# Spectral filter with a two-layer network on one core: two last-stage pieces moved, the first batch's x in five loads, the filter's downward rows first

## The chip, the core and the metric

The kernel runs on one core of a Trainium2 chip. A core has five engines that run at the same time, each with its own list of instructions, and that wait for one another through semaphores: PE (TensorE: matrix products, its weight loads shown apart as PEld), DVE (VectorE), ACT (ScalarE), POOL (GpSimd) and SP (SyncE, here only an issuer of transfers). PE writes into PSUM, a small memory of eight banks; DVE and ACT copy from there to SBUF, the working memory. Transfers between DRAM and SBUF are issued by SP or POOL and carried out by 16 DMA engines. The metric is the time of one execution on the device in microseconds (us).

## The reference

`x` has 8 batches of 3008 positions and 256 channels. It is filtered in the frequency domain along the positions and then sent through a two-layer network with a leaky activation:

```python
X = np.fft.rfft(x, axis=1)
Y = X * (filt_r + 1j * filt_i)[None, :, :]
y = np.fft.irfft(Y, n=x.shape[1], axis=1)
g = y.reshape(B * S, D) @ w_in                      # 256 -> 2048
g = np.maximum(g, 0.0) + alpha * np.minimum(g, 0.0)
out = g @ w_out                                     # 2048 -> 256
```

## The kernel before, in words

The transform of length 3008 = 94 * 32 is done as two layers of small matrix products, and so is its inverse. Matrix operands are fp16; `x` and the filter are turned from fp32 to fp16 by the DMA that loads them, and only POOL issues such DMAs.

The network (`class Block`) takes 512 positions at a time (one block of each pair of batches has 384). `up` multiplies by `win_s` into a two-bank PSUM tile `hps`; ACT copies it to `gtb` (L569; L591 in `up4`), and DVE makes `m` (L572, L596) and adds it to `gtb` (L574, L597). `down` multiplies by `wout_s` (L614); ACT copies to `osb`, SP stores. A block is 16 steps, each one `up` and as a rule one unit of `down`. Into these steps the FFT work of the following batches is put by a plan written out by hand: `put(step, fn, ...)` puts a piece ahead of the `up` of that step. The first block has no `down` work yet. It is done as two halves of 256 positions by `up4`: eight calls, at steps 0, 2, ..., 14, the first four for the first half and the last four for the second. `up4` takes functions (`mid`) that are called between its matmuls and its ACT copy.

The first batch has nothing to hide behind, so `class First` does its FFT ahead of the blocks, in this order:

- `load_x` (L116) brings x of a batch in four parts `c` of eight positions each, into four `xs` buffers with 94 rows (partitions) of 2048 values; each part is two DMAs of 48 and 46 rows. `load_filt` (L136) brings the filter in three loads of four of the twelve frequency pairs `kp`, each as eight DMAs: real and imaginary part, two groups `e`, and 16 rows read upward (one contiguous run a row) or 16 rows read downward (step -1, eight runs a row).
- `piece_a(i)`, i = 0 to 7, is the first layer (L337): two pieces for each part `c`. ACT and DVE copy the results to `am`, which is a part of `gtb`.
- `turn_at` (L351) transposes two to four columns of `am` on PE; a copy brings them to `at`.
- `piece_b(kp)` (L363) is the second layer; DVE multiplies its result by the filter, `uu(kp)` (L368). It uses one `hps` buffer, of which there are two, so DVE's products set the pace of `piece_b`.
- `piece_c(kp)` (L389) starts the inverse; `keep_c` copies its result to `v` after every second pair, and after each of the last two.
- `side_t`, `half_t` and `piece_t` (L411, L405) transpose `v` on PE, and a copy brings it to `zt`.
- `half_d` and `pair_d` (L288) are the last stage of the inverse: eight matmuls of `wif_s` for a `pair_d`, four for a `half_d`, and a copy to `yT`, the input of the network. `half_d(0)` to `half_d(3)` give the first 752 positions and `pair_d(2)`, `pair_d(3)` the next 752, one half of the channels each. `pair_d` uses `psF`, a PSUM tile of which there is one buffer.

`warm(n, bank)` (L452) puts n matmuls of the identity into PE's list, whose results nobody reads; they fill PE's time. Each has one weight load and 512 columns.

The transfers of the network's weights `win_s` and `wout_s` and of x of the second batch are issued by POOL in the loop over `kp`, at `kp == 4`; the first of them waits for a DVE memset on `win_s`, which stands behind `uu(6)` in DVE's list. POOL's DMAs take eight semaphores in turn, so that each waits until the DMA eight places earlier has landed.

Of the kernel before, what the change touches and what calls it, by code (L numbers as in the profile page):

```python
# [14 lines left out]
N1 = 94  # L15
N2 = 32
NK = 24
D = 256
# [37 lines left out]
def kernel(  # L56
# [10 lines left out]
    nc = tc.nc  # L67
# [28 lines left out]
    filt_s = konst.tile([128, 12, 2, D], FP16, name="filt_s")  # L96
# [15 lines left out]
    def xrow(b, c):  # L112
        return bass.AP(tensor=x.tensor, offset=x.offset + (b * NFFT + 8 * c) * D,
                       ap=[[N2 * D, N1], [1, 8 * D]])

    def load_x(b, c, held=False):  # L116
        xs = p_x.tile([128, 8 * D], FP16, name="xs")
        if held:
            for r in (slice(0, 32), slice(64, 96)):
                nc.vector.memset(xs[r, 0:2], 0.0)  # L120
        for r in (slice(0, 48), slice(48, N1)):
            nc.gpsimd.dma_start(out=xs[r], in_=xrow(b, c)[r])  # L122
        return xs

    def load_halves(b, c):
# [7 lines left out]
            nc.gpsimd.dma_start(out=hi[32:47], in_=xrow(b, c)[79:94])  # L133
        return lo, hi

    def load_filt(eng, dst, ha, hb, parts=(0, 1)):  # L136
        n = hb - ha
        for i in parts:
            src = (filt_r, filt_i)[i]
            for e in range(2):  # L140
                q = 64 * e + 32 * i
                k = 2 * ha + 24 * e
                for j, step, off in ((0, 1, k), (16, -1, N1 - k)):
                    eng.dma_start(  # L144
                        out=dst[q + j : q + j + 16, ha:hb].rearrange("p h r d -> p (h r) d"),
                        in_=bass.AP(tensor=src.tensor, offset=src.offset + off * D,
                                    ap=[[N1 * D, 16], [step * D, 2 * n], [1, D]]))

    def banks(wide):
        if wide:  # L150
            return psH.tile([128, 2, 512], FP32, name="hps")
        return psF.tile([128, 2, 512], FP32, name="psF")

    def bank(kind):
        if kind == "o":
            return psO.tile([128, 2, D], FP32, name="op").rearrange("p k d -> p (k d)")
        return banks(kind == "h")[:, 0]
# [151 lines left out]
    def on_act(o, i):  # L309
        nc.scalar.activation(o, i, AF.Copy)  # L310

    def on_dve(o, i):
        nc.vector.tensor_copy(o, i)  # L313
# [116 lines left out]
    def table(ka, kb):  # L430
        nc.sync.dma_start(out=twf_s[:, ka:kb], in_=consts["twf"].ap()[:, ka:kb])

    def inverse_table(ka, pb):
        for i in range(4):
            nc.tensor.matmul(pb[:, 128 * i : 128 * i + 128],
                             twf_s[:, ka + 2 * i : ka + 2 * i + 2].rearrange("p k m -> p (k m)"), id16,
                             start=True, stop=True)
        on_act(twi_s[:, ka : ka + 8].rearrange("p k m -> p (k m)"), pb)

    def swapped(ka, eng):  # L440
        t, o = twi_s[:, ka : ka + 8], twx_s[:, ka : ka + 8]
        eng.tensor_scalar(o[:, :, 32:64], t[:, :, 0:32], gs_s, None, OP.mult)
        eng.tensor_scalar(o[:, :, 0:32], t[:, :, 32:64], gs_s, -1.0, OP.mult, OP.mult)

    xc = {(0, c): load_x(0, c) for c in range(4)}
    f0 = First()
    table(0, 8)
    load_filt(nc.gpsimd, filt_s, 0, 4)

    def warm(n, pw):  # L450
        for _ in range(n):
            nc.tensor.matmul(pw.rearrange("p (r c) -> p r c", r=4), id16,  # L452
                             id16.unsqueeze(1).to_broadcast([128, 4, 128]), start=True, stop=True)

    warm(10, bank("o"))
    for i in range(8):
        f0.piece_a(i, i % 3 < 2)
        if i == 3:
            inverse_table(0, bank("o"))
            swapped(0, nc.vector)  # L460
            warm(3, bank("o"))
        elif i % 2 == 1:
            warm((8, 0, 6, 0)[i // 2], bank("o"))
        if i in (5, 7):
            ka = 4 * i - 12
            nc.vector.memset(twf_s[:, ka : ka + 8, 0:1], 0.0)
            table(ka, ka + 8)
    load_filt(nc.gpsimd, filt_s, 4, 8)
    warm(3, bank("o"))
    f0.turn_at(0, 1, on_act)  # L470
    f0.turn_at(1, 1, on_dve, True)
    warm(2, bank("o"))
# [1 line left out]
    f0.turn_at(2, 2, on_act)  # L474
    f0.piece_b(1)
    inverse_table(8, bank("o"))
    load_filt(nc.gpsimd, filt_s, 8, 12)
    nc.gpsimd.memset(twi_s[:, 16:24, 0:1], 0.0)
    swapped(8, nc.gpsimd)
    nc.gpsimd.tensor_copy(id32, ids[0:16, 0:16])  # L480
# [7 lines left out]
    nc.sync.dma_start(out=twi_s[:, 16:24], in_=consts["twj"].ap())  # L488
    nc.sync.dma_start(out=twx_s[:, 16:24], in_=consts["twy"].ap())
    for kp in range(12):  # L490
        if 0 < kp < 9:
            f0.piece_b(kp + 2)
        if kp == 8:
            f0.piece_b(11)
        if kp == 4:
            nc.vector.memset(win_s[:, :, 0:1], 0.0)
            for kt in range(2):
                nc.gpsimd.dma_start(out=win_s[:, kt], in_=moe_w_in[kt * 128 : (kt + 1) * 128])
            xc[(1, 0)] = load_x(1, 0)
            for q in range(2):  # L500
                nc.gpsimd.dma_start(
                    out=wout_s[:, 8 * q : 8 * q + 8],
                    in_=moe_w_out[1024 * q : 1024 * q + 1024].rearrange("(j p) d -> p j d", p=128))
            for c in range(1, 4):
                xc[(1, c)] = load_x(1, c)
        f0.piece_c(kp)
        if kp > 9:
            f0.keep_c(kp, (on_act, on_act) if kp == 10 else both, 1)
        elif kp % 2 == 1:
            f0.keep_c(kp - 1, (on_act, on_act))  # L510
            if kp < 7:
                f0.turn_at(kp + 5, 2, on_act)
        if 7 < kp < 10:
            warm(2, banks(False)[:, 0])
    for o in range(0, 128, 64):
        for i in range(0, 64, 32):
            nc.gpsimd.dma_start(out=filts_s[o + i : o + i + 32], in_=filt_s[o + 32 : o + 64])
# [3 lines left out]
    on_act(*f0.side_t(0))  # L521
    on_dve(*f0.side_t(1))
    later = [f0.half_t(2, "h"), f0.half_t(3, "f")]
    f0.half_d(0, on_dve, "o")
    f0.half_d(2, on_act, "o")

    sizes = [512] * 5 + [384] + [512] * 6
    blocks = []
# [96 lines left out]
    def put(step, fn, *args):  # L625
        plan.setdefault(step, []).append((fn, args))
# [41 lines left out]
    put(1, f0.piece_t, 2, on_dve)  # L668
    for i in (6, 7):
        put(3, lambda i=i: on_dve(*f0.half_t(i, "o")))  # L670
    put(5, f0.pair_d, 2, on_dve)
    put(7, f0.pair_d, 3, on_dve)
    for g, ts, ds, te, de in ((2, (19, 23), (25, 28), (on_dve, on_dve), (on_dve, on_dve)),
                              (3, (32, 34), (43, 49), (on_act, on_act), (on_act, on_act))):
        for i in range(2):
# [16 lines left out]
    for b in range(3, NB):  # L692
        p = 96 * (b - 1)
# [20 lines left out]
    for step in range(16):  # L714
        if step % 2 == 0:
            blk.up4(step // 2 % 4, step // 8,
                    [] if step else [lambda: on_dve(*later[0]), lambda: on_act(*later[1]), slopes])
        for fn, args in plan.pop(step, ()):
            fn(*args)
    blk.start_down(False)  # L720
    units.extend((blk, q) for q in range(16))
    step = 16

    for p, t0, tn in blocks[1:]:
        blk = Block(p, t0, tn)
        for j in range(16):
            n = psum.get(step, 0)
# [50 lines left out]
```

## Time and profile before

| | us |
|---|---|
| median of 3 runs (770.80 to 771.02) | 771.01 |
| the profiled execution | 771.15 |
| its span, first to last instruction | 769.4 |
| PE busy in the span (99%) | 758.3 |
| DVE busy (82%) | 633.5 |
| ACT busy (76%) | 582.7 |
| POOL busy (19%) | 147.0 |

The profile gives the span of one execution. A timeline row has the start and the busy time in us, the engine, the line, the operation with what it writes and reads, the count of merged instructions, and in brackets the idle time ahead of it with what ended that. A row of the chain of waits has the start, the duration and what the end of the program goes back to at that time. "issue" is time in which an engine waited for nothing that the profile shows. The table gives busy time by stage, from the view by windows:

| stretch, us | PE | DVE | ACT | POOL | granted clock |
|---|---|---|---|---|---|
| 0 to 15: x, first layer | 12.55 | 4.63 | 5.22 | 10.18 | 1.00 |
| 15 to 31: second layer, filter, inverse | 13.46 | 14.37 | 11.08 | 13.25 | 1.00 |
| 31 to 35: to the first `up4` | 3.63 | 2.25 | 2.50 | 0.66 | 1.00 |
| 35 to 43: first block | 7.54 | 5.44 | 5.87 | 2.85 | 1.00 |
| 43 to 57: first and second block | 13.31 | 13.83 | 12.20 | 2.75 | 1.00 |

### The profile page before, as it was taken

Reading aid. Unit: us, or ns where it says so; the run is one execution under the profiler, and the core shown is the slowest. Engines: PE = TensorE matmul, PEld = TensorE weight load, DVE = VectorE, ACT = ScalarE, POOL = GpSimd, SP = SyncE. Lnnn points to the kernel's source line nnn. Section 1 sums busy time; section 2 is a strip of 40 time slices with the busy share of each in tenths; the row PEclk is TensorE's granted clock in tenths of the full one; section 3 lists DMA queues with packets and bytes.
Section 4 is the critical chain, followed back from the end, with each engine's and each line's share of the span. In section 5 each row is a group of like instructions: output and inputs, shape, how many; then the busy total and the mean of one; then the engine's idle time right before and its main releaser. Section 6 shows DMA issues by size and latency. Waiting matters only on the chain.

```text
span 769.4 us, 16586 instructions
## 1 busy us (share of the span) xinstructions
PE 758.3 (99%) x6544; PEld 507.4 (66%) x6544; DVE 633.5 (82%) x1160; ACT 582.7 (76%) x670; POOL 147.0 (19%) x278
## 2 busy tenths in 40 slices
PE   8999999999999999999999999999999999999998
PEld 4666667666666666666666666766666666766666
DVE  3888885889889998899978998999877888666663
ACT  3787788888778787887778777787767777776664
POOL 7621560122211211121202222022101212000000
PEclk9999999999999999999999999999999999999999
DMA  9996896664843549533783538644463223510111
GB/s 158 165 233 166 138 209 193 168 169 122 201 133 90 138 130 197 153 87 93 187 217 83 132 101 173 178 98 118 125 159 94 69 71 96 152 36 28 42 42 56
DMA packets 97150, 100.04 MB, mean 130 GB/s; under 512 B 12100, under 2 KB 83412, under 8 KB 96880
## 3 DMA queue, kind: packets, MB, share of 16 engines
q1 hardware_dynamic: 82384, 69.50, 31.2%
q0 software_dynamic: 14688, 29.49, 21.3%
q8 instruction: 51, 0.84, 0.4%
q14 instruction: 27, 0.22, 0.1%
HBM read 55.02 MB, written 46.66 MB: 132 GB/s over the span
## 4 chain that ended last, share of the span: by engine, by line
PE 92%; DVE 3%; DMA 2%; ACT 1%; POOL 1%; issue 1%; ACTq 0%; DVEq 0%; POOLq 0%
PE op L614 42%; PE hps L560 41%; PE psF L288 3%; PE hps L266 2%; PE psF L235 1%; DMA xs<-in_x_dram 1%; PE hps L181 1%; PE hps L207 1%; DVE gtb L597 1%; DVE zt L313 1%; ACT asb L310 1%; DVE m L596 1%; DMA filt_s<-in_filt_r_dram 1%; POOL filt_s L144 1%; DMA filt_s<-in_filt_i_dram 1%
## 5 line engine op out<-in xcount | busy, mean ns | idle before, releaser
L569 ACT ACTIVATE gtb<-hps 128x1024 f16<-128x1024 f32 (+1 forms) x376 | 377.6, 1007 | 134.3 <-PE hps L560 130.5
L614 PE MATMUL op<-wout_s,gtb 128*128 128x256 f16 x3008 | 431.3, 273 | 0.0
L560 PE MATMUL hps<-yT,win_s 128*128 128x512 f16 (+1 forms) x1504 | 418.4, 375 | 0.9 <-ACT asb L310 0.3
L614 PEld LDWEIGHTS <-gtb 128*128 128x128 f16 x3008 | 290.9, 98 | 164.2 <-issue 10.7
L572 DVE TENSOR_SCALAR m<-gtb,alm_s 128x512 f16<-128x512 f16 (+1 forms) x752 | 226.9, 345 | 99.4 <-ACT gtb L569 98.0
L574 DVE TENSOR_TENSOR gtb<-gtb,m 128x2048 f16<-128x2048 f16 (+1 forms) x188 | 226.1, 1202 | 10.4
L560 PEld LDWEIGHTS <-win_s 128*128 128x128 f16 x1504 | 142.4, 98 | 55.2 <-issue 6.0
L249 POOL DMA_DIRECT2D sw<-ww x144 | 71.6, 506 | 414.5 <-DVE ww L242 408.7
L619 ACT ACTIVATE osb<-op 128x512 f32<-128x512 f32 (+1 forms) x97 | 56.6, 583 | 12.3 <-PE op L614 10.9
L310 ACT ACTIVATE asb<-hps 128x1024 f16<-128x1024 f32 (+1 forms) x56 | 56.6, 1019 | 5.6 <-PE hps L181 4.3
L310 ACT ACTIVATE v<-hps 128x1024 f16<-128x1024 f32 (+1 forms) x43 | 43.4, 1010 | 10.8 <-PE hps L266 10.6
L242 DVE TENSOR_TENSOR ww<-psF,filts_s 128x1024 f16<-128x1024 f32 x42 | 51.1, 1217 | 0.2 <-PE psF L235 0.2
L243 DVE TENSOR_TENSOR uu<-psF,filt_s 128x1024 f16<-128x1024 f32 x42 | 51.0, 1213 | 0.0
L310 ACT ACTIVATE yT<-psF 128x752 f16<-128x752 f32 x58 | 46.1, 795 | 2.0 <-PE psF L288 1.9
L288 PEld LDWEIGHTS <-zt 96*128 96x128 f16 x512 | 28.5, 98 | 7.2 <-issue 1.2
L288 PE MATMUL psF<-wi_s,zt 96*128 96x94 f16 x448 | 27.9, 205 | 0.1
L247 POOL DMA_DIRECT2D uu<-ww x24 | 19.7, 1241 | 31.5 <-DVE uu L243 23.3
L254 DVE TENSOR_TENSOR uu<-uu,sw 128x1024 f16<-128x1024 f16 x36 | 24.5, 681 | 0.6 <-issue 0.4
L122 POOL DMA_DIRECT2D xs<-in_x_dram x32 | 21.7, 910 | 13.2 <-PE hps L560 4.9
L191 DVE TENSOR_TENSOR xs<-xs 47x2048 f16<-47x2048 f16 x16 | 19.5, 1219 | 0.4
L195 DVE TENSOR_TENSOR xs<-xs 47x2048 f16<-47x2048 f16 x16 | 19.3, 1209 | 0.0
L266 PE MATMUL hps<-uu,twi_s 64*64 64x256 f16 x336 | 17.3, 281 | 0.0
(93 smaller groups left out, 259.9 us busy)
## 6 DMA issues: line engine op xcount, KB each, us to landing
out_dram<-osb SPq DMA_DIRECT2D x128, 128.0 KB
v_dram<-v SPq DMA_DIRECT2D x84, 128.0 KB
zt<-v_dram SPq DMA_DIRECT2D x28, 384.0 KB
sw<-ww POOLq DMA_DIRECT2D x144, 64.0 KB, 2.6
xs<-in_x_dram POOLq DMA_DIRECT2D x44, 192.0 KB, 6.4
at<-a_dram SPq DMA_DIRECT2D x40, 192.0 KB
a_dram<-asb SPq DMA_DIRECT2D x32, 192.0 KB
a_dram<-asb SPq DMA_DIRECT2D x12, 384.0 KB
```

Source lines behind the costliest of these rows:

```text
L242: nc.vector.tensor_mul(ww, px, fs)
L243: nc.vector.tensor_mul(uu, px, f)
L249: nc.gpsimd.dma_start(out=sw[o : o + 32], in_=ww[i : i + 32])
L266: nc.tensor.matmul(ps[64 * par : 64 * par + 64, e, 256 * h : 256 * h + 256], twi_s[r, 4 * q + 2 * h + par], u[r, par, h], start=True, stop ...
L288: nc.tensor.matmul(ps[:, m], self.zt[:, 8 * g + 4 * mh + m, dh * 128 : dh * 128 + 128], self.wi, start=True, stop=True)
L310: nc.scalar.activation(o, i, AF.Copy)
L560: nc.tensor.matmul(self.hps[:, j % 2, 0:tn], win_s[:, kt, j * 128 : (j + 1) * 128], yT[:, kt, self.t0 : self.t0 + tn], start=(kt == 0), st ...
L569: nc.scalar.activation(g[:, 2 * i : 2 * i + 2], self.hps[:, :, 0:tn], AF.Copy)
L572: nc.vector.tensor_scalar(m[:, 2 * i + h], g[:, 2 * i + h], 0.0, a, OP.min, OP.mult)
L574: nc.vector.tensor_add(g, g, m)
L614: nc.tensor.matmul(self.op[:, si - s0], self.gts[k][:, 128 * si : 128 * si + 128], wout_s[:, k], start=(si == s0 and k == 0), stop=(si == ...
L619: nc.scalar.activation(osb[:, 0:m], self.op[:, 0:m], AF.Copy)
```

## The change

It consists of these edits:

1. x of the first batch comes in five DMAs instead of eight: all 94 rows at once, parts 0 to 2 whole and part 3 in two halves of the columns, so that `piece_a(6)` needs only the first of them. The other batches keep the two DMAs of 48 and 46 rows.
2. `load_filt` issues the four DMAs of the downward rows first and then the four of the upward ones; before, they took turns.
3. Four matmuls of `warm` go in the first layer and behind it (6 to 3, and 3 to 2), and four in the loop over `kp` (two each at `kp` 8 and 9).
4. `piece_b(11)` stands at `kp == 9`, behind `piece_c(8)`; before, it stood at `kp == 8` ahead of it.
5. The copies of `half_d(0)` and `half_d(2)` exchange engines: ACT has the first now, DVE the second.
6. `pair_d(2)` goes from step 5 to step 7, behind the fourth `up4`. `pair_d(3)` goes from step 7 into `mid` of the fifth `up4` (step 8), behind that one's matmuls and ahead of its ACT copy. Both are copied by DVE, as before.

```diff
@@ load_x
-        for r in (slice(0, 48), slice(48, N1)):
-            nc.gpsimd.dma_start(out=xs[r], in_=xrow(b, c)[r])
+        if b:
+            for r in (slice(0, 48), slice(48, N1)):
+                nc.gpsimd.dma_start(out=xs[r], in_=xrow(b, c)[r])
+        else:
+            w = 8 * D // (1 + (c == 3))
+            for o in range(0, 8 * D, w):
+                nc.gpsimd.dma_start(out=xs[0:N1, o : o + w], in_=xrow(b, c)[:, o : o + w])
@@ load_filt
-    def load_filt(eng, dst, ha, hb, parts=(0, 1)):
-        n = hb - ha
-        for i in parts:
-            src = (filt_r, filt_i)[i]
-            for e in range(2):
-                q = 64 * e + 32 * i
-                k = 2 * ha + 24 * e
-                for j, step, off in ((0, 1, k), (16, -1, N1 - k)):
-                    eng.dma_start(
-                        out=dst[q + j : q + j + 16, ha:hb].rearrange("p h r d -> p (h r) d"),
+    def load_filt(ha, hb):
+        for j, step, base in ((16, -1, N1), (0, 1, 0)):
+            for i, src in enumerate((filt_r, filt_i)):
+                for e in range(2):
+                    q = 64 * e + 32 * i + j
+                    off = base + step * (2 * ha + NK * e)
+                    nc.gpsimd.dma_start(
+                        out=filt_s[q : q + 16, ha:hb].rearrange("p h r d -> p (h r) d"),
                         in_=bass.AP(tensor=src.tensor, offset=src.offset + off * D,
-                                    ap=[[N1 * D, 16], [step * D, 2 * n], [1, D]]))
+                                    ap=[[N1 * D, 16], [step * D, 2 * (hb - ha)], [1, D]]))
@@ first layer
-            warm((8, 0, 6, 0)[i // 2], bank("o"))
+            warm((8, 0, 3, 0)[i // 2], bank("o"))
...
-    warm(3, bank("o"))
+    warm(2, bank("o"))
     f0.turn_at(0, 1, on_act)
@@ loop over kp
-        if 0 < kp < 9:
+        if 0 < kp < 10:
             f0.piece_b(kp + 2)
-        if kp == 8:
-            f0.piece_b(11)
...
-        if 7 < kp < 10:
-            warm(2, banks(False)[:, 0])
@@ ahead of the blocks
-    f0.half_d(0, on_dve, "o")
-    f0.half_d(2, on_act, "o")
+    f0.half_d(0, on_act, "o")
+    f0.half_d(2, on_dve, "o")
@@ plan
-    put(5, f0.pair_d, 2, on_dve)
-    put(7, f0.pair_d, 3, on_dve)
+    put(7, f0.pair_d, 2, on_dve)
@@ first block
             blk.up4(step // 2 % 4, step // 8,
-                    [] if step else [lambda: on_dve(*later[0]), lambda: on_act(*later[1]), slopes])
+                    {0: [lambda: on_dve(*later[0]), lambda: on_act(*later[1]), slopes],
+                     8: [lambda: f0.pair_d(3, on_dve)]}.get(step, []))
```

More of the change, by code (lines that the diff above doesn't have):

```diff
@@ L447 @@
     table(0, 8)
-    load_filt(nc.gpsimd, filt_s, 0, 4)
+    load_filt(0, 4)
     def warm(n, pw):
@@ L467 @@
             table(ka, ka + 8)
-    load_filt(nc.gpsimd, filt_s, 4, 8)
-    warm(3, bank("o"))
+    load_filt(4, 8)
+    warm(2, bank("o"))
     f0.turn_at(0, 1, on_act)
@@ L476 @@
     inverse_table(8, bank("o"))
-    load_filt(nc.gpsimd, filt_s, 8, 12)
+    load_filt(8, 12)
     nc.gpsimd.memset(twi_s[:, 16:24, 0:1], 0.0)
```

## The prediction, made before the changed kernel was run

> **What bounds the kernel now.** I read the page first, then the chain of waits over 0 to 110 us, then the timeline of the first 60 us engine by engine.
>
> ```profile
> PE 758.3 (99%) x6544; PEld 507.4 (66%) x6544; DVE 633.5 (82%) x1160; ACT 582.7 (76%) x670; POOL 147.0 (19%) x278
> PE   8999999999999999999999999999999999999998
> PEclk9999999999999999999999999999999999999999
> ```
>
> PE is dense in all slices but the first and the last, at full clock. What the change can win lies before the dense part, as an earlier arrival at it; afterwards the same matmuls follow. The chain of waits says what sets that arrival:
>
> ```profile
> 4.96 7.57 DMA xs<-in_x_dram
> ...
> 12.82 1.00 POOL filt_s L144 x2
> ...
> 25.94 0.68 DVE uu L368
> ...
> 42.66 1.15 DVE m L596 x4
> ...
> 57.16 0.49 PE psF L288 x8
> ```
>
> Up to 12.5 us it is the x transfer, then filter transfers, then the filter products `uu` on DVE, a mixed stretch of PE, ACT and DVE, DVE to 57.16, then PE. Two rows of the timeline fix the first joint:
>
> ```profile
> 12.82 0.53 POOL L144 DMA_DIRECT2D filt_s<-in_filt_i_dram  x1 [0.46 <-DMA xs<-in_x_dram]
> ...
> 16.87 9.15 DVE L368 TENSOR_TENSOR uu<-hps,filt_s 128x1024 f16<-128x1024 f32 x8 [1.09 <-PE hps L363]
> ```
>
> The eighth filter DMA is issued at 12.82, when the eighth x DMA has landed (12.53); it lands 3.9 us after issue, at 16.7, and DVE starts `uu(0)` at 16.87. The row names PE, but its `hps` was done at 15.92: the last releaser is the filter. From there twelve products run 1.14 us apart without a gap and end at 30.55.
>
> **Part 1: loads and the first filter load.** POOL's DMAs wait for the one eight places earlier (with eight x loads, filter k waits for x k). With five x loads, filters 1 to 3 wait for nothing, and the eighth waits for x load 5, the last. POOL saves three issues of 0.54 us (L122), at nothing: x is bound by the transfer (1.0 us a load against 0.54 of issue); uncovered they would be worth 1.6. Bytes are the same, and a 48-row and a 46-row load give most engines three packets each, a 94-row load six. So the last x lands at 12.5 again (12.4 to 12.7; the last two loads have 2 KB rows), and the eighth filter is again issued at 12.8. What changes is what it is: an upward one, one 4 KB packet (0.32 us in the packet records) per engine instead of eight of 512 B (0.06 each, 0.48), with the seven before it in the queue earlier. Its first engines cannot land before 15.1, as now (issue plus 2.3); only the tail to 16.7 can shrink. (The Trainium skill, "DMA: Bandwidth & Descriptors", on the anatomy of one DMA, fits about 2.0 us plus bytes over 436 GB/s; as an estimate by that page 64 KB lands 2.15 after issue, at 15.0, and part 1 would be worth its cap. The trace has 3.9 in this place, behind a full queue, and 2.3 for the earliest engine alone, so the row decides.) I take 16.1, a gain of 0.6, between the bounds 0 (same tail) and 1.45 (landing at 15.3).
>
> PE must be ready too. Piece 6 now needs only the first half of the last x (11.6 instead of 12.53) and six filler matmuls become three (1.28 to 0.64 us, so 11.52 to 12.16); piece 7 starts at about 12.6 instead of 13.2. Transposes and `piece_b(0)`, now ending at 15.92, end at about 15.3: in time for 16.1. The fourth dropped filler lies in this cover; without it, it would be worth its own 0.2.
>
> Is the next thing late? `uu(4)` would start at 20.8 and needs the second filter load, which lands at 20.8 now (issue 17.03 plus 3.8); `uu(8)` at 25.3 needs the third, at 25.2 (21.36 plus 3.9). Both follow by 0 to 0.3 us, since POOL issues them back to back. They cap the gain at about 0.6 to 0.9. **I take 0.6.**
>
> **Part 2: end of the product stage.** `piece_b(11)` moves behind `piece_c(8)` (32 weight loads and matmuls together, one product; no DMA) and four fillers go. The order of the work on DVE and ACT stays. The rows:
>
> ```profile
> 29.90 0.60 PE L452 MATMUL psF<-ids 128*128 128x512 f16 x2
> ...
> 31.99 0.50 PEld L411 LDWEIGHTS <-v 128*96 128x96 f16 x8 [0.53 <-ACT v L310]
> ...
> 34.58 0.33 PEld L583 LDWEIGHTS <-win_s 128*128 128x128 f16 x4 [0.18 <-DMA win_s<-in_moe_w_in_dram]
> ```
>
> The fillers on `psF` end at 30.50, so `piece_c(10)` runs only at 30.56, though `uu(10)` is done at 29.4; its two copies hold ACT (31.00 to 31.66) ahead of the last `v` copy (31.55 to 31.94), for which PE waits at 31.99. Without the fillers `piece_c(10)` is over and copied before `uu(11)` ends; the last `v` copy then runs at about 31.04 to 31.43, and the transposes start at 31.48: 0.5 earlier. Exchanging the two `half_d` copies puts ACT's 0.48 us in DVE's place (0.55) before the first `up4`: 0.07. Together 0.57 at the first `up4` matmul.
>
> But its second half needs `win_s`, second part, which lands at 34.5 (25.82 plus 8.7) and already holds PE for 0.18. That load is released by a DVE memset behind `uu(6)`, so it moves by part 1's 0.6 and by nothing of part 2. Wanted at 34.40 (34.58 less the wait) - 0.6 - 0.57 = 33.2, there at 33.9: a new wait of 0.7, with `slopes`, `half_d(1)`, `half_d(3)` and `piece_t(2)` queued behind it on PE. If all of it holds, part 2 gives 0. It gives up to 0.57 if that tail shrinks: a 16 KB instruction fetch of 0.97 us at 32.52 lies in it, and that moves with PE. **I take 0.2**, nearer to the row as it stands.
>
> **Part 3: the two last-stage pieces.** Each is 8 weight loads, 8 matmuls and a DVE copy of 0.94; no DMA.
>
> ```profile
> 38.43 0.74 PE L288 MATMUL psF<-wif_s,zt 96*128 96x94 f16 x8
> 39.00 1.04 PE L583 MATMUL hps<-yT,win_s 128*128 128x256 f16 x8
> 40.20 0.49 PE L288 MATMUL psF<-wif_s,zt 96*128 96x94 f16 x8 [0.15 <-DVE yT L313]
> ...
> 42.66 1.14 DVE L596 TENSOR_SCALAR m<-gtb,alm_s 128x512 f16<-128x512 f16 x4 [0.99 <-ACT gtb L591]
> ```
>
> Now `pair_d(2)` waits on PE for DVE's `zt` (38.87) with `up4(3,0)` queued behind. Moved, on the old clock: `up4(3,0)` at 38.43; `pair_d(2)` 39.30 to 39.82, its copy to 40.76; `up4(0,1)` 39.68 to 40.72 and its ACT copy 40.74 to 41.76 (now 41.60 to 42.63). `pair_d(3)` then holds PE until `psF` is free at 40.76, with the other `up4` of the half behind it; matmuls to 41.29, copy to 42.25. DVE's first `m` comes at 42.27 instead of 42.66: 0.39. The ACT copies behind (0.96 apart, five to the end of the second `asb` copy) begin at 42.2 instead of 42.54: 0.34. PE is dense from 45.3, so the lesser counts: **0.35**, bounds 0.1 (the wait on `psF` eats more) and 0.5.
>
> Sum: 0.6 + 0.2 + 0.35 = 1.15 us. From 45 us on PE idles for only 0.3 us at 46.65 and 0.3 at 57.16, both behind ACT and DVE rows that move too, so the shift reaches the end. The profiled execution took 771.15 (span 769.4, 1.75 around it), 0.14 above the median 771.01: 771.15 - 1.15 = 770.0, in a median 769.9. This is **same** by 0.2% (1.54 us, about what a measurement of this kernel can tell from no change).
>
> **Rivals.**
> A, all three gains in full: the filter's tail goes (0.9, its cap), `win_s` comes in time (0.5), part 3 gives 0.45: 1.85, median 769.2. For it: the late landings at 16.7 and 34.5 are each one engine's (the other fifteen are there by 15.94 and 32.98), and instruction fetches stand beside both. Against: the last engine sets the semaphore, and the fetches still come.
> B, transfer hidden nowhere: the eighth filter still lands at 16.7, since it is issued at the same 12.8; then `win_s` does not move either, and part 3 alone is left: 770.7. Loads and order would not do what they seem to.
> C, slower: PE's clock. Eight fillers go, four of them at 29 to 31 us. Place: 31 to 35 us, where PE is busy 3.63 of 4.00. If the granted clock falls to one half there for that stretch, its rows take up to 3.6 more; 1.15 gained leaves +2.5, median 773.5. It decides as soon as a slice of that stretch shows less than 1.00. Against: 17 to 31 us has PE busy 11.49 of 14.00 with a gap of 1.0 at 17.2, at 1.00; the fillers' places leave gaps of under 1.0. The Trainium skill ("TensorE: Matmul & The Clock Gate", Part 1) says that an idle window of about 3.4 us halves the clock. No row of this trace shows such a gap after PE's first matmul, so by that rule C stays out too.
> D, slower: 94 rows run on few engines. On two engines, from 3.0 on, 47 packets of 0.32 make 15.2 us for the first load, PE starts at 18.2 instead of 6.65, and the sum is +10.4, median 781.4. It decides at the first x landing. Against: the 46-row loads, as awkward a number, land 1.0 us after the 48-row ones. The Trainium skill ("DMA: Bandwidth & Descriptors", on why a DMA increments its semaphore by 16) has the engines be the largest divisor up to 16 of the row count, two for 94, with exceptions for POOL's loads; it would say two for 46 as well, and the trace disagrees.
>
> **How the numbers follow.** Forecast 0.55, with its own range 769.4 to 770.4; A 0.24; B 0.14; C 0.04; D 0.03. Faster by over 0.2% (below 769.47): A and a fifth of the forecast, 0.35. Slower: C and D, 0.07. The rest, 0.58, is within. The range runs from somewhat below A's 769.2 (part 1's other bound adds 0.5) to above B: 768.7 to 771.0; it leaves out C, D and a little of A and B.
>
> **What would show it.** Part 1: first `uu` at 16.2 to 16.4, the last at 30.0, no gap at the fifth and ninth. Part 2: transposes of `v` 1.1 earlier, then a wait of PE on `win_s`, 0.2 to 0.7 long. Part 3: first `m` of `up4` 1.1 earlier. I am wrong if `uu` has gaps, if `uu(0)` starts before 16.0 or after 16.7, or if PE has new waits after 57 us that give the shift back.

## The result and the profile after

The changed kernel takes 769.82 us (median of 16 executions, 769.16 to 770.74), the kernel before 770.97 in the same series (16 executions): ratio 0.9983, 95% interval 0.9977 to 0.9990. The interval lies on both sides of the 0.998 that the prediction took as the limit of what can be told. The profiled execution took 769.81 (span 768.0, 1.4 less than the 769.4 of before), so the profile can stand for the median.

The first view is the page, engines and slices:

```profile
PE 757.2 (99%) x6536; PEld 507.5 (66%) x6536; DVE 633.5 (82%) x1160; ACT 582.8 (76%) x670; POOL 145.7 (19%) x275
PE   8899999999999999999999999999999999999998
PEclk9999999999999999999999999999999999999999
```

Eight matmuls and three DMA issues fewer, and the same dense PE: what was won is an earlier arrival at the dense part (from the first DVE `m` of the first block to the end of the span it is 726.71 us before and 726.73 after). The chain of waits of the changed kernel (start, duration, what):

```profile
2.52 4.45 PE op L455 x10
6.96 1.28 PE hps L340 x16
8.24 1.77 PE op L455 x8
...
15.43 0.41 PE hps L366 x16
...
25.03 8.59 DMA win_s<-in_moe_w_in_dram
...
33.67 0.61 PE hps L582 x4
...
41.31 1.14 DVE m L595 x4
```

Before, 7.57 us of the x transfer stood in this place. Now it is mostly PE up to 15.43, and the transfer is no longer last: the ten matmuls of `warm` at 2.52 took 0.445 us each, the eight at 8.24 took 0.22, and the trace's record of the granted clock begins at 8.20 (ahead of it the page has no record, and shows full clock). Then the chain goes through the transfer of `win_s`, which landed at 33.62. The first DVE `m` of the first block comes at 41.31 instead of 42.66. Rows of the timeline (start, busy time, engine, line, what it writes and reads):

```profile
12.17 0.49 POOL L147 DMA_DIRECT2D filt_s<-in_filt_i_dram  x1 [0.47 <-DMA xs<-in_x_dram]
...
15.43 0.41 PE L366 MATMUL hps<-at,twf_s 64*32 64x256 f16 x16
...
15.91 9.32 DVE L371 TENSOR_TENSOR uu<-hps,filt_s 128x1024 f16<-128x1024 f32 x8 [0.21 <-DMA filt_s<-in_filt_r_dram]
...
25.15 4.61 DVE L371 TENSOR_TENSOR uu<-hps,filt_s 128x1024 f16<-128x1024 f32 x4
...
30.83 0.50 PEld L414 LDWEIGHTS <-v 128*96 128x96 f16 x8 [0.35 <-ACT v L313]
...
33.66 0.33 PEld L582 LDWEIGHTS <-win_s 128*128 128x128 f16 x4 [0.50 <-DMA win_s<-in_moe_w_in_dram]
```

The last x landed at 11.89 (12.53 before), the eighth filter DMA went out at 12.17 (12.82) and landed at 14.72 (16.75). So the bracket of the fourth row may not be taken at its word: it names the filter, which had been there for 1.2 us, while PE's `hps` ended at 15.84. The last releaser is PE, just as in before the bracket named PE and the filter was last. The last `uu` ends at 29.76 (30.55), the transposes of `v` start at 30.83 (31.99): 1.07 behind it instead of 1.45. Then PE waits 0.50 for the second part of `win_s`.

### The profile page after: what moved, and what is told of

Its sections match the earlier page's. It is cut to its first block, busy times and chain, and to the rows that moved or that the text cites. A ratio compares the mean times of both kernels' runs of the same rounds, so it can differ in the third digit from the quotient of the medians.

```text
span 768.0 us, 16563 instructions
## 1 busy us (share of the span) xinstructions
PE 757.2 (99%) x6536; PEld 507.5 (66%) x6536; DVE 633.5 (82%) x1160; ACT 582.8 (76%) x670; POOL 145.7 (19%) x275
## 4 chain that ended last, share of the span: by engine, by line
PE 94%; DVE 2%; ACT 2%; DMA 1%; issue 0%; POOL 0%; ACTq 0%
PE op L613 42%; PE hps L559 41%; PE psF L291 3%; PE hps L269 2%; PE psF L238 1%; DMA win_s<-in_moe_w_in_dram 1%; PE op L455 1%; PE hps L184 1%; PE hps L210 1%; DVE gtb L596 1%; ACT asb L313 1%; DVE m L595 1%; PE hps L582 0%; ACT gtb L568 0%; DVE zt L316 0%
## 5 line engine op out<-in xcount | busy, mean ns | idle before, releaser
L123 POOL DMA_DIRECT2D xs<-in_x_dram x24 | 17.5, 1012 | 12.2 <-PE hps L559 4.8
```

## The experiments

Every run is compared with the kernel before on the same chip (770.97 to 771.07 there). Executions of one kernel differ in one more thing, the mean granted clock over the span. In some it is 0.998 or less. Two profiles caught such an execution: in both the clock was at one half for 3.41 us, and the mean was 0.998. Executions with such a mean are counted as "fallen" and are part of each median; the median of the others stands beside it. A mean of 0.999 is not counted: in the profile of before, which has it, the clock was at one half only from 768.27 on, behind PE's last matmul (765.91).

| kernel | median (executions) | ratio to before, 95% | fallen | median of the others |
|---|---|---|---|---|
| before, all series after the first | 771.01 (103) | | 12 | 770.98 |
| changed, first series | 769.82 (16) | 0.9977 to 0.9990 | 5 | 769.68 |
| the same, second series | 769.77 (11) | 0.9976 to 0.9993 | 5 | 769.62 |
| the same, third series | 770.33 (11) | 0.9982 to 0.9999 | 7 | 769.68 |
| loads alone | 770.47 (11) | 0.9982 to 0.9999 | 1 | 770.43 |
| end of the product stage alone | 771.49 (11) | 0.9994 to 1.0012 | 6 | 771.1 |
| pieces alone | 770.63 (11) | 0.9984 to 1.0001 | 0 | 770.63 |

### The three parts, each alone

`p1_loads_only` has edits 1 and 2 and the four fillers of the first layer:

```diff
+            for o in range(0, 8 * D, w):
+                nc.gpsimd.dma_start(out=xs[0:N1, o : o + w], in_=xrow(b, c)[:, o : o + w])
...
+        for j, step, base in ((16, -1, N1), (0, 1, 0)):
...
-            warm((8, 0, 6, 0)[i // 2], bank("o"))
+            warm((8, 0, 3, 0)[i // 2], bank("o"))
...
-    warm(3, bank("o"))
+    warm(2, bank("o"))
```

> Part 1 alone: x of the first batch in five loads, downward filter rows first, the fillers of the first layer 6 to 3 and 3 to 2; nothing else. Theory (the parts add, and win_s comes with the DVE memset): the eighth filter load lands at about 14.7 instead of 16.7, the first uu starts at 15.7 to 16.0 when PE is ready, uu ends at 29.7 to 29.9 instead of 30.55, win_s's second half lands 0.8 earlier too, and the kernel gains 0.7 to 0.9 us against before. Rival (the loads are hidden by what follows, the gain is in the later parts): uu ends earlier but the first m stays at 42.6, gain 0.0 to 0.2.

`p2_end_only` has the loop's edits and the exchanged copies:

```diff
-        if 0 < kp < 9:
+        if 0 < kp < 10:
             f0.piece_b(kp + 2)
-        if kp == 8:
-            f0.piece_b(11)
...
-        if 7 < kp < 10:
-            warm(2, banks(False)[:, 0])
...
-    f0.half_d(0, on_dve, "o")
-    f0.half_d(2, on_act, "o")
+    f0.half_d(0, on_act, "o")
+    f0.half_d(2, on_dve, "o")
```

> Part 2 alone: piece_b(11) behind piece_c(8), the four fillers of the loop out, the two half_d copies exchanged. Theory (win_s takes the place of what is removed): transposes of v start at 31.5 to 31.7 instead of 31.99, then PE waits 0.5 to 0.7 us for win_s's second half, which stays at 34.5; the first m comes 0.0 to 0.1 earlier, gain 0.0 to 0.1 us. Rival (the transfer comes in time): no wait of over 0.3, gain 0.4 to 0.57 us.

`p3_pieces_only` has edit 6 alone:

```diff
-    put(5, f0.pair_d, 2, on_dve)
-    put(7, f0.pair_d, 3, on_dve)
+    put(7, f0.pair_d, 2, on_dve)
...
+                     8: [lambda: f0.pair_d(3, on_dve)]}.get(step, []))
```

> Part 3 alone: pair_d(2) behind the fourth up4, pair_d(3) inside the fifth. Theory: nothing moves before 38 us, the first m comes at 42.2 to 42.3 instead of 42.66, gain 0.35 to 0.45 us. Rival (PE's wait on psF holds the next up4 and eats it): first m earlier, but the second asb copy and the dense part not, gain 0.0 to 0.1 us.

Measured: loads 0.6 below the kernel before (forecast 0.7 to 0.9 there), pieces 0.4 below (its interval just reaches 1), the end of the product stage nothing or a loss (its profile has no wait for `win_s`, which was the rival's condition, but the rival's 0.4 did not come either). The profiles say more than the times, since stretches with fixed work are the same in every one of them:

| stretch, us | before | with the part | gain | in the profiles of |
|---|---|---|---|---|
| last `uu` end to transposes of `v` | 1.45 | 1.07 | 0.38 | before, loads, pieces / end, changed and several below |
| `uu(10)` end to transposes of `v` | 2.57 to 2.58 | 2.20 to 2.21 | 0.37 | before, loads, pieces / end, changed and six more |
| transposes to first `up4` matmul | 2.09 | 2.02 | 0.07 | the same |
| first `up4` to first `m`, without a wait on `win_s` | 8.50 to 8.51 | 8.06 | 0.44 | loads, end / pieces and six more |

The timeline of `p3_pieces_only` has `m` at 41.77, though its first `up4` was at 33.71:

```profile
33.71 1.03 PE L583 MATMUL hps<-yT,win_s 128*128 128x256 f16 x8 [0.32 <-DVE yT L313]
...
41.77 1.13 DVE L596 TENSOR_SCALAR m<-gtb,alm_s 128x512 f16<-128x512 f16 x4
```

8.06 against 8.50 of the loads and 8.51 of the end; before has 8.58 (34.08 to 42.66) with its wait of 0.18 on `win_s`. That is part 3, and it needs no other part. The loads move the beginning: of the nine profiles with the new loads and filter order the last `uu` ends at 29.81 on average (29.33 to 30.55), of the three with the old ones at 30.31 (30.18 to 30.55). That is part 1: 0.50, from few profiles that are up to 1.2 us apart. And part 2 does take 0.45 off the path in the profile, but 6 of its 11 executions had the fallen clock (medians 771.71 with, 771.1 without), against 12 of 103 of the kernel before. The five others do not show the 0.45 either (771.1 against 770.98). Its profile lost 0.21 of the gain again between 76 and 98 us: from the first `m` to the end it has 726.95, the thirteen other profiles 726.69 to 726.76. Why is not shown.

### Which of the two edits of the loads, and the transfer of win_s

`e5_old_order` is the changed kernel with the filter's DMAs taking turns as before, `e6_eight_x` the changed kernel with x in eight DMAs, `e4_win_earlier` has the transfers of the network's weights one product earlier:

```diff
-        for j, step, base in ((16, -1, N1), (0, 1, 0)):
-            for i, src in enumerate((filt_r, filt_i)):
-                for e in range(2):
+        for i in parts:
+            for e in range(2):
+                for j, step, off in ((0, 1, k), (16, -1, N1 - k)):
```

> The changed kernel with five x loads, but the filter's upward and downward rows in turns as before. In the profiles so far the last of the first eight filter loads landed at 16.75, 16.24 and 15.32 with the old loads and at 14.72, 15.62 and 14.66 with the new ones; the first uu started at 16.3 to 16.9 and 15.5 to 16.0. Theory O (the order matters: the last load is one packet an engine instead of eight): it lands 0.3 to 0.7 later than with the new order, at 15.3 to 16.0. Rival F (five loads matter: x ends earlier and the filters are in the queue earlier): 14.7 to 15.6, as with the new order. Time: O 0.2 to 0.5 us above the changed kernel, F the same.

```diff
-            for o in range(0, 8 * D, w):
-                nc.gpsimd.dma_start(out=xs[0:N1, o : o + w], in_=xrow(b, c)[:, o : o + w])
+        for r in (slice(0, 48), slice(48, N1)):
+            nc.gpsimd.dma_start(out=xs[r], in_=xrow(b, c)[r])
```

> The changed kernel with x in eight loads as before and the new order of the filter rows. Theory O (the order matters): the eighth filter load lands at 15.0 to 15.5. Rival F (the five loads matter): the last x lands at 12.2 to 12.6 and the eighth filter load at 15.3 to 16.8, the first uu at 16.2 to 16.8, time 0.4 to 0.8 us above the changed kernel.

```diff
-        if kp == 4:
+        if kp == 3:
             nc.vector.memset(win_s[:, :, 0:1], 0.0)
```

> The changed kernel with the memset and the loads of win_s, wout_s and the second batch's x at kp 3 instead of 4, one product (1.14 us) earlier. Theory (in the changed kernel win_s is the wait that eats part 2): win_s's second half lands at about 32.5, PE's wait of 0.5 before the first up4's second half goes, everything behind comes 0.3 to 0.45 earlier, 769.4 against 769.8. Rival (another wait takes its place: the copies of zt and yT, or the third filter load delayed by the new traffic, seen as a gap before the ninth uu): gain 0.0 to 0.1 or a loss.

Measured: 769.98 (0.9974 to 0.9996), 769.99 (0.9973 to 0.9991) and 769.50 (0.9969 to 0.9986); without the fallen executions 769.63, 769.89 and 769.49, where the changed kernel has 769.66. Neither edit of the loads is needed by itself: five loads in the old order had the eighth filter DMA in at 14.66, as rival F says, and eight loads in the new order at 15.41, as theory O says (with both as before 16.75, 16.24 and 15.32 in three profiles, the new pair 14.64 to 15.63). What the two have in common shows at the fifth product; `e5_old_order`:

```profile
15.47 4.62 DVE L373 TENSOR_TENSOR uu<-hps,filt_s 128x1024 f16<-128x1024 f32 x4 [0.21 <-PE hps L368]
20.83 4.63 DVE L373 TENSOR_TENSOR uu<-hps,filt_s 128x1024 f16<-128x1024 f32 x4 [0.74 <-DMA filt_s<-in_filt_r_dram]
```

DVE begins at 15.47 and has to wait 0.74 for the second filter load; a start of 15.9 would have come to nearly the same at 20.8. This is the cap that the prediction named. Seven of the eleven profiles with five loads or the new order have such a wait, 0.17 to 0.80 long. In the others the second load came in time, and there the early start was kept: `e4_win_earlier` has it in at 19.46 and ends its last `uu` at 29.33. How much of the earlier landing of the eighth DMA is order and how much is the number of loads stays open.

`e4_win_earlier` was repeated as `e4_win_again`, in one series with the changed kernel unchanged (`after_again`).

> The changed kernel once more, beside the next one on the same chip. Theory (the time is the start of the first uu plus fixed stretches): last uu to transposes of v 1.07 us, transposes to first up4 2.02, first up4 to first m 8.06 plus what PE waits for win_s (0 to 0.5), m to the end as before; the median 769.6 to 770.1 with the first uu between 15.4 and 16.1. Rival (the gain of the first profile was a lucky draw of the loads): first uu after 16.3 and a median above 770.4.

> The changed kernel with the loads of the network's weights one product earlier, once more, beside the changed kernel on the same chip. Theory (win_s's second half comes late in a part of the executions, where one engine is held up): no wait of PE for win_s, median 0.1 to 0.45 us below the changed kernel. Rival (the wait was of one profile only, and what the first run showed was its earlier first uu): the same time within 0.1 us.

Measured: 769.77 for the changed kernel; 770.55 (0.9982 to 1.0002) for the earlier transfer, 7 of 11 fallen, 769.43 for the others. The gain of the first series did not come again in the median, and 0.2 among the executions at full clock is what may be left of it. The wait on `win_s` is 0.50 in the changed kernel's first profile and 0.52 in that of `e11_fillers_back` below; there is none in those of loads, end, pieces, old order or eight x. The second and third profile of the changed kernel have none either, but they caught fallen executions, in which PE comes 1 us later. From issue to landing the second part took 7.03 to 8.95 us over the fourteen profiles: in seven of them the last of the 16 engines was 0.85 to 1.73 behind the fifteenth, in the seven others 0.3 or less.

### Where the clock falls

The profile of `after_again` is one of a fallen execution, 771.43 with a span of 769.7. The view by windows around it (stretch: us, PE busy, PEld, DVE, ACT, POOL, the granted clock, DMA share, GB/s):

```profile
27.05:30.46 3.41, 2.23 (x92) 1.35 (x84) 3.41 (x4) 2.06 (x5) 2.74 (x4) 1.00 1.06 208
30.46:33.87 3.41, 3.26 (x33) 2.40 (x34) 0.88 (x3) 1.64 (x5) 0.52 (x1) 0.50 1.04 202
```

The clock is 0.50 from 30.46 to 33.87, which but for half a microsecond is the place of rival C (31 to 35). Here is what it does to the path in the timeline:

```profile
31.15 1.46 PE L455 MATMUL hps<-ids 128*128 128x512 f16 x3
...
32.40 1.06 PE L414 MATMUL op<-ids,v 128*96 128x128 f16 x8
...
34.91 1.03 PE L582 MATMUL hps<-yT,win_s 128*128 128x256 f16 x8 [0.32 <-ACT yT L313]
```

The three fillers behind the loop take 1.46 instead of 0.82 and hold the transposes, which start at 31.98 (their first weight load), 1.43 behind the last `uu` (30.55) instead of 1.07; from there to the first `up4` it is 2.93 instead of 2.02. 0.36 + 0.91 = 1.27 us, and the first `up4` is at 34.91, 0.8 later than before any change. The window ahead of the fall has PE busy 2.23 of 3.41, two thirds, with no gap of over 0.8 us.

Two questions were left: whether the loop's fillers are what holds the clock, and what they cost on the path. `e11_fillers_back` puts them where they were; `e10_fillers_moved` puts five matmuls where PE waits for DVE anyway, two ahead of the product of `kp` 8 and three behind that of `kp` 10; `e12_win_and_fillers` adds the earlier `win_s`; `after_third` is the changed kernel once more, in the same series.

```diff
+        if 7 < kp < 10:
+            warm(2, banks(False)[:, 0])
     for o in range(0, 128, 64):
```

> The changed kernel with the loop's four fillers back where they were, at the ends of kp 8 and 9. Theory C: the clock falls in at most 2 of 11 executions; full-clock executions 0.2 to 0.4 us above the changed kernel (piece_c(10) waits behind the fillers, transposes 0.3 later), so a median of 769.8 to 770.1, the same as the changed kernel's. Rival: falls as often as in the changed kernel, median 0.3 above it.

```diff
+        if kp == 8:
+            warm(2, banks(False)[:, 0])
...
+            if kp == 10:
+                warm(3, bank("h"))
```

> The changed kernel with five filler matmuls put into PE's idle gaps of the loop: two ahead of piece_c(8), three between piece_c(10) and piece_c(11). So far the granted clock fell for one stretch (run mean 0.998 or lower) in 30 of 83 executions of kernels without the loop's fillers, in 11 of 90 with them; each such execution is 0.7 to 1.9 us longer. Theory C (the gate answers to PE's idle time in 26 to 30 us): at most 2 of some 11 executions with a fallen clock; those at full clock at 769.5 to 769.8, as the changed kernel; median 769.5 to 769.8. Rival (the fall has nothing to do with the fillers, it is chance or the chip): 3 to 6 of 11 again. Rival 2 (the fillers hold piece_c(11) up): full-clock executions 0.2 or more above the changed kernel.

> The five fillers in PE's gaps and the loads of the network's weights one product earlier, together. Theory: few falls of the clock, no wait for win_s, full-clock executions at 769.3 to 769.5, median 769.3 to 769.6, 0.2 to 0.5 below the changed kernel. Rival (the gains do not add): median within 0.1 of the better of the two alone.

> The changed kernel as it is, on the same chip as the three before. Theory C: the clock falls in 3 to 6 of some 11 executions, those at 770.4 to 771.4, the others at 769.4 to 769.9; median 769.6 to 770.4. Rival (chance or the chip): as rare as in the kernels with fillers here, 0 to 2.

| kernel | median (executions) | ratio to before, 95% | fallen | median of the others |
|---|---|---|---|---|
| fillers back | 769.89 (12) | 0.9991 to 1.0000 | 2 | 769.85 |
| fillers moved | 769.71 (11) | 0.9973 to 0.9990 | 0 | 769.71 |
| fillers moved, `win_s` earlier | 769.54 (11) | 0.9976 to 0.9994 | 1 | 769.53 |
| changed kernel, third series | 770.33 (11) | 0.9982 to 0.9999 | 7 | 769.68 |

The profile of `after_third` is a fallen one again, that of the moved fillers is not. First `after_third`:

```profile
26.01:29.42 3.41, 2.10 (x82) 1.31 (x80) 3.36 (x3) 2.20 (x5) 3.13 (x5) 1.00 0.95 185
29.42:32.84 3.42, 3.41 (x35) 2.55 (x36) 0.94 (x2) 1.50 (x4) 1.05 (x2) 0.50 1.05 211
```

Then `e10_fillers_moved`, whose clock was granted at 6.57 as in `after_again`, so that the same stretch can be laid beside it:

```profile
27.05:30.46 3.41, 3.13 (x94) 1.66 (x87) 2.97 (x3) 2.14 (x6) 2.87 (x5) 1.00 1.08 210
30.46:33.87 3.41, 3.14 (x36) 2.23 (x35) 2.08 (x4) 1.94 (x4) 0.96 (x2) 1.00 1.03 201
```

PE was busy 3.13 instead of 2.23 there, and the clock held. Over all series the changed kernel fell in 17 of 38 executions, the other kernels without the loop's fillers in 20 of 56 (from 1 of 12 to 7 of 11), those that have them at either place in 4 of 56 (loads 1, pieces 0, back 2, moved 0, moved with `win_s` 1), the kernel before in 12 of 103. So the fillers make the falls rare: in the shared series, 7 of 11 without them stand against 2 of 12 with them at the old place and 0 of 11 at the new one. What the 12 falls of the kernel before are, some 1.9 long in the time, stays open, since no profile caught one. In the changed kernel a fall costs 0.8 in the median (770.48 fallen, 769.66 not), and 17 of 38 of that is some 0.4 in the mean.

At full clock the fillers' old place costs about 0.2 (769.85 against 769.66), the new place nothing that shows. The profile of `e11_fillers_back` has the price at the last product:

```profile
24.82 3.48 DVE L371 TENSOR_TENSOR uu<-hps,filt_s 128x1024 f16<-128x1024 f32 x3
...
28.06 0.41 PE L366 MATMUL hps<-at,twf_s 64*32 64x256 f16 x16
...
28.55 1.23 DVE L371 TENSOR_TENSOR uu<-hps,filt_s 128x1024 f16<-128x1024 f32 x1 [0.24 <-PE hps L366]
...
30.84 0.50 PEld L414 LDWEIGHTS <-v 128*96 128x96 f16 x8 [0.35 <-ACT v L313]
```

The fillers at `kp` 8 now stand ahead of `piece_b(11)` and hold `uu(11)` by 0.24. The transposes start 1.06 behind the last `uu` (29.78), as without fillers, but only because that product is late itself. Counted from the end of the product before it, `uu(10)`, at 28.30, they start 2.54 behind; before it was 2.58 (29.41 to 31.99), in the changed kernel 2.20 (28.62 to 30.83), and as much with the moved fillers. So the stretch owes 0.34 of its 0.37 to the fillers' going from this place. The move of `piece_b(11)` is worth the other 0.04 while they stand there; no run has the fillers out and this piece at its old place. All executions together, the kernel with the moved fillers has a mean of 769.67 and the changed kernel of 770.07: 0.40 less, 95% interval 0.13 to 0.68, over series on several chips. In the series that they share, the medians are 0.62 apart. It is the better version of the two; beside the kernel before it is 0.9982 (0.9973 to 0.9990).

## Why the prediction held, and where its steps did not

Forecast 769.9 (768.7 to 771.0), "same" by 0.2% as the likeliest; measured 769.82 and, over all 38 executions, 769.87. The mechanism of all three parts is as forecast. That the total is so near is in part luck: the sum leaves out the clock, whose loss is some 0.4 against 0.2 before, and has part 1 too high by 0.1 and parts 2 and 3 too low by 0.3.

| step | forecast gain | measured | from |
|---|---|---|---|
| part 1, loads | 0.6 (0 to 1.45, cap 0.6 to 0.9) | 0.50 | last `uu`, nine profiles against three |
| part 2, end of the product stage | 0.2 (0 to 0.57) | 0.45 where `win_s` is in time, about 0 with the wait of 0.50 (first `up4` to first `m` 8.46 instead of 8.06); nothing in the time of this part alone | fixed stretches |
| part 3, pieces | 0.35 (0.1 to 0.5) | 0.44 | first `up4` to first `m` |
| sum | 1.15 | 1.3 at full clock (770.98 to 769.66) | executions without a fall |
| clock (rival C) | nothing, chance 0.04 | a loss of 0.8 in 17 of 38 executions | windows, fallen executions |

1.3 at full clock less some 0.4 for the falls, against 0.2 of the same in the kernel before (12 of 103 falls of 1.9 each): means 771.21 and 770.07, 1.14 apart.

**Part 1: right in size, wrong in its course.** "So the last x lands at 12.5 again": it landed at 11.55 to 12.46, 11.89 in the changed kernel's profile. With five DMAs the last x landed at 11.9 on average (ten profiles), with eight at 12.4 (four): the same bytes came in earlier in fewer DMAs. The eighth filter DMA was expected at 16.1 and landed at 14.6 to 15.6. By the prediction's own test (`uu(0)` before 16.0) the step was wrong: 15.91 in the changed kernel's profile, 15.2 to 16.05 in the others with its loads. The Trainium skill ("DMA: Bandwidth & Descriptors", the anatomy of one DMA) fits about 2.0 us plus the bytes over 436 GB/s, 2.15 for this DMA; the trace has 2.55 (12.17 to 14.72), nearer to it than to the 3.9 that the prediction preferred. Over the nine profiles of the new loads it is 2.55 to 3.23, between the two. The row of 3.9 was one draw: the same DMA of the old loads took 2.84 in the profile of the pieces alone (12.48 to 15.32), and 3.35 in that of the end alone. So the prediction took its gain from a landing that was late by chance, which makes the size in part luck; what held it near was that the next thing late was named rightly: the second filter load, seen as waits of 0.17 to 0.80 at the fifth product in seven profiles; "no gap at the fifth" did not hold in those.

**Part 2: the gain there, its cause right but for a row overlooked, the wait only sometimes there.** The transposes come 0.37 nearer to the products (forecast 0.5), the exchanged copies give the 0.07. The prediction put the 0.5 on the fillers on `psF` ahead of `piece_c(10)`, and with the fillers back 0.34 of it was lost again. What it overlooked is that ACT was busy from 30.00 to 31.94 without a break, so that an earlier `piece_c(10)` alone would not have been copied earlier. In the kernel before, `piece_b(11)` waited for a free `hps` until 28.34, with `piece_c(8)` queued behind it on PE to 28.68, though `uu(8)` was done at 27.1 (16.87 and nine products of 1.14); then came two fillers (29.02 to 29.62) and only then `piece_c(9)`, though `uu(9)` was done at 28.28:

```profile
28.34 0.41 PE L363 MATMUL hps<-at,twf_s 64*32 64x256 f16 x16 [0.72 <-DVE uu L368]
...
28.68 0.29 PEld L389 LDWEIGHTS <-uu 64*128 64x128 f16 x16 [0.20 <-issue]
...
29.02 0.60 PE L452 MATMUL psF<-ids 128*128 128x512 f16 x2
...
30.00 1.08 ACT L310 ACTIVATE v<-op 128x512 f16<-128x512 f32 x2 [2.02 <-PE op L389]
```

ACT stood idle for 2.02 ahead of the copies of `piece_c(8)` and `piece_c(9)`, and the later copies of `v` came right behind them. These first copies began 0.59 after the end of `uu(10)`, 0.55 after it with the fillers back, and 0.14 ahead of it in the changed kernel. That ACT's copies are what bounds the transposes is argued from these rows; that the fillers' place sets the stretch is shown by the runs. The wait on `win_s` was forecast at 0.7 and was 0.50 in one of the changed kernel's three profiles. So the fillers' old place cost 0.34 on the path in the profile (0.2 in the medians at full clock), and their loss brings rival C.

**Part 3: right.** 0.44 against 0.35. The wait of `pair_d(3)` on `psF` was as short as forecast: the matmuls ahead of it on PE ended at 39.82, DVE's copy at 39.86, and its own began at 39.92.

**Rival C: dismissed for the wrong reason.** The place (31 to 35 us) and the mechanism were right, the chance of 0.04 and the price of 3.6 were not. The reasons against were that an earlier stretch with PE busy 11.49 of 14.00 kept its clock and that no gap was over 1.0 us. That is 0.82 on average; what the two falls followed were windows of 0.62 and 0.65, without a long gap. The profile of before could not show them: in its own steps of 3.41 us, counted from the grant at 7.09, PE is busy 2.64 (0.77) in the step ahead of that place (27.57 to 30.98), and the lowest of its steps up to 57 us is 2.50 (0.73, 17.33 to 20.74). The Trainium skill ("TensorE: Matmul & The Clock Gate", Part 1) has an idle window of about 3.4 us halve the clock. The length agrees with the trace: the fall lasts 3.41 us, and the window ahead of it is of the same length. But PE was not idle in it. It was busy for two thirds, and the measurement decides. The price was too high because the prediction kept the clock down for all the work of the stretch: the fall ends after 3.41 us, in which PE at half clock does 1.7 us of work at most, so that no more than 1.7 can be lost. It was 1.27 in the profile.

**Rivals A, B and D.** D is out: the first part of x landed at 6.18 (its two loads by 6.55 before) and the last at 11.89 (12.53), earlier, not later. B is out: the eighth filter DMA landed at 14.72 instead of 16.75. A (1.85, median 769.2) asked for everything in full; the lowest executions, 769.1, are there, but part 1 did not give its 0.9 on average.

## What to carry to other kernels

Filler matmuls on a path are not only a delay. Before taking them out, count PE's busy share in windows as long as the clock's own step (3.4 us here), not the gaps; where it would come near two thirds with many small matmuls, as in both falls here, move the fillers into PE's waits instead of dropping them. One profile at full clock does not show that a kernel keeps its clock; the mean clock of every execution does. And when a transfer is made earlier, look up which transfer is next: here it took back up to 0.8 us of what the first one gained.

## What the runs showed of the hardware beyond that

- The clock goes up and down in steps of 3.41 us. It was granted at 5.3 to 8.2 us after the start, another time in each execution. Both recorded falls came 23.89 us after the grant, seven steps of 3.41 (30.46 and 29.42); in the twelve other profiles it stayed up until behind PE's last matmul, 761.17 or 764.59 us, which is 223 or 224 such steps. Which stretch of the work falls into one step so depends on the execution, and with it whether the same kernel falls.
- The busy share of PE in a step does not tell alone whether the clock falls behind it. Counted in each profile's own steps up to 57 us, the falls followed the two lowest, 0.62 and 0.65; the next, 0.68 in `e4_win_again`, was followed by none. But at the end of the program the clock stayed up behind steps with 0.53 to 0.62 in five profiles, as in that of the changed kernel:

```profile
27.23:30.64 3.41, 2.31 (x82) 1.48 (x81) 2.88 (x4) 2.23 (x6) 1.70 (x4) 1.00 1.06 208
...
762.54:765.95 3.41, 2.02 (x19) 1.56 (x16) 0.00 (x0) 0.77 (x2) 0.00 (x0) 1.00 0.35 115
765.95:768.03 2.08, 0.00 (x0) 0.00 (x0) 0.00 (x0) 0.00 (x0) 0.00 (x0) 1.00 0.18 63
```

The first row is of `e4_win_again`, the others of the changed kernel. The 2.02 us at the end are 19 matmuls of 128 by 128 with 256 columns without a gap; the steps ahead of the falls have 82 and 92 matmuls, most of them of 64 rows. Whether it is their size that counts is not shown.

- A transfer here has a spread of its own: the second part of `win_s` took 7.03 to 8.95 us from issue to landing, and up to 1.73 of that was one late engine of 16.
